# A two-stage feed-forward kernel on one Trainium2 core: the second stage's second product with its weights stationary and 512 tokens moving

## The chip, the cores and the metric

The kernel runs on one core of a Trainium2 chip. The metric is device time in microseconds of one launch; the layout of inputs before it and of outputs after it is done by the host and isn't in the time.

## What is computed

Three blocks follow each other; all data is float32.

```python
# attention without softmax, 4 x 8 heads of 576 tokens x 64
kv = einsum('bhsd,bhse->bhde', k, v)
out = einsum('bhsd,bhde->bhse', q, kv)
x = out / sqrt(mean(out * out, -1) + 1e-6) * g_norm      # -> 2304 tokens x 512
# first stage: 512 -> 1536 -> 512
x = ((x @ w_a) * (x @ w_b)) @ w_out
# second stage: 512 -> 2048 -> 512
h = x @ w_in
g = maximum(h, 0) + log1p(exp(-abs(h)))                  # softplus
return g @ w_out2
```

The change is in the last line, `g @ w_out2`.

## The kernel before

**Tokens in blocks.** The 2304 tokens are cut into five blocks. Blocks 1 to 4 are the first 512 tokens of each of the four sequences; block 0 (256 tokens) gathers the remaining 64 of each. Activations lie transposed in SBUF: features on the 128 partitions, tokens along the free axis.

**Three products for one.** Every float32 product is made of three `fp32r` products: each operand is split into a high half (ScalarE, `half_hi`, L166) and a low half, operand minus high half (VectorE, `half_lo`, L169), and `P3 = ((0, 0), (0, 1), (1, 0))` names the pairs (half of the weight, half of the operand) that are multiplied: high by high, high by low, low by high. A split tile is `[P, 2, 512]`: half, then column.

**The second stage in pairs.** Blocks 1 and 2 form pair 0, blocks 3 and 4 pair 1. Each pair is multiplied by the scheme of Strassen and Winograd with seven products of half size in place of eight. `stage1` (L608, products at L591) computes h in eight rounds i (`NCP` = 8), with `soft` for the softplus, and leaves the tiles `g2[i]`; `g_sums` on GpSimd adds and subtracts some of them. After all eight rounds of a pair, `stage2_2` (L674) does the second product. In pair 1 the rounds also hold block 0's products: `single1` (L787) and `single2` (L815), the latter through `sums` (L768).

**The stage that the change touches.** `stage2_2` runs over 56 steps: seven turns (`TURNS`: A11, S2, A12, S3, S1, A22, S4) of eight steps `cp` each. A step has one operand tile (512 tokens x 128 features, split; written by `operand`, L680) and one weight tile (128 features x 256 outputs, split). The turns add up in pairs of PSUM banks: A11 and A12 in set "a", S2, S3 and A22 in set "b", S1 and S4 in set "c". In a step the operand is the stationary side: 128 of its tokens are loaded at a time, the 256 weight columns are moved past them, and this is done for four groups of tokens (`i2`) by three halves, 12 products of 256 columns. Bank b of a set holds the tokens of groups 2b and 2b+1, 256 columns each; tokens are on the partitions of the result, as the output wants them:

```python
for i2 in range(NK):
    b, k = i2 // 2, i2 % 2
    for q, (a, c) in enumerate(P3):
        nc.tensor.matmul(out=set_[where][b][:, k * 256:(k + 1) * 256],
                         lhsT=x[:, c, i2 * P:(i2 + 1) * P], rhs=w[:, a, :], ...)
```

At the last step of a turn `leave` (L719) reads each bank out: a copy on ScalarE (L709, turns A11 and A12) or a sum with a kept tile on VectorE (L704, the others); turns A12, S1, A22 and S4 store the result by `store` (L712), two tiles of 256 KB each, in rows of 256 outputs.

**What sets the order.** Up to the first stage's start a script fixes each engine's order (`SCRIPT`); the stages behind it are written as generators, and the framework's scheduler orders each engine's instructions from what they need and from the order in which they were written. Operands are written three steps ahead (`AHEAD`). The weight tiles come from device memory, where the kernel has put the split weights (`kept`): `t_load` (L665) issues two transfers of 256 KB for two steps, on SP's queue, a turn ahead. The stores are on SP's queue too, in one row with the loads. Beside pair 0's steps `op_steps(1)` (L466) makes the operands of pair 1's first product, from step 9 to step 53 (`OPS_AT`): its sums are L480 to L482 and L499.

Of the kernel before, what the change touches and what calls it, by code (L numbers as in the profile page):

```python
# [9 lines left out]
F32 = mybir.dt.float32  # L10
# [6 lines left out]
P = 128  # L17
B, S, D = 4, 576, 64
NT = B * S
DM = 512  # L20
NK = DM // P
# [11 lines left out]
N = 512  # L33
REST = S - N
# [5 lines left out]
NCP = F2 // 2  # L40
# [70 lines left out]
def attention_gated_softplus_kernel(  # L111
# [9 lines left out]
    w2_in: bass.AP,  # L121
    w2_out: bass.AP,
    out: bass.AP,
):
    nc = tc.nc
    const = ctx.enter_context(tc.tile_pool(name="const", bufs=1))
# [13 lines left out]
    def t2(shape, dt=F32, what="t2"):  # L140
        return t2pool.tile(shape, dt, tag="t2", name=nm(what))
# [4 lines left out]
    def bank(what):  # L146
        return accp.tile([P, 512], F32, tag="acc", name=nm(what))

    def t4(shape, dt, what):
        return big.tile(shape, dt, tag="big", name=nm(what))  # L150
# [20 lines left out]
    def split(hi, lo, src):  # L171
        half_hi(hi, src)
        half_lo(hi, lo, src)
# [342 lines left out]
    def keep_steps(cp):  # L516
# [18 lines left out]
        def last(items, k, to):  # L535
# [8 lines left out]
            lambda: w_value(h[1]),  # L544
            lambda: keep((cp, 1), h[1]),
            lambda: sums(h, True),
            lambda: last(h, 0, 2),
            lambda: (last(h, 1, 2), w_load(o[0])),
# [3 lines left out]
            lambda: w_value(o[1]),  # L552
            lambda: keep((cp, 5), o[1]),
            lambda: sums(o, False),
            lambda: last(o, 0, 6),
            lambda: last(o, 1, 6),
# [108 lines left out]
    def t_load(k, half, cps):  # L665

        t = t4([P, 2, 2, 256], F32R, "w2o")
        for n, cp in enumerate(cps):
            nc.sync.dma_start(
                out=t[:, n].bitcast(F32), in_=kept_w[cp, k][:, :, half * 256:(half + 1) * 256]  # L670
            )
        return t

    def stage2_2(pair, beside):  # L674

        j1, j2 = PAIRS[pair]
        steps = [(n, cp) for n in range(len(TURNS)) for cp in range(NCP)]
        halves2, weights, set_, kept_s = {}, {}, {}, {}

        def operand(n, cp):  # L680
            name = TURNS[n][0]
            i = pair * NCP + cp
            (a11, a12), (a21, a22) = g2[i]

            src = {"A11": a11, "S2": a11, "A12": a12, "S3": a21, "A22": a22, "S4": a12}
            src = s1g[i] if name == "S1" else src[name]
            t = halves2[n, cp] = t4([P, 2, 512], F32R, "op2")
            split(t[:, 0], t[:, 1], src)
            if name == "A11":
                nc.vector.tensor_tensor(out=a11, in0=s1g[i], in1=a11, op=ALU.subtract)  # L690
            if name == "A12":
                nc.vector.tensor_tensor(out=a12, in0=a12, in1=a11, op=ALU.subtract)
            if name == "S1":
                s1g.pop(i)
            if name == "S4":
                g2.pop(i)

        def load(n, cp):
            if n < len(TURNS):
                weights[n, cp] = t_load(TURNS[n][1], TURNS[n][2], (cp, cp + 1))  # L700

        def plus(a, b):
            t = t2([P, 512], what="s2")
            nc.vector.tensor_tensor(out=t, in0=a, in1=b, op=ALU.add)  # L704
            return t

        def copy(a):
            t = t2([P, 512], what="c2")
            nc.scalar.activation(out=t, in_=a, func=AF.Copy)  # L709
            return t  # L710

        def store(j, half, b, t):  # L712
            r = (j - 1) * S + b * 2 * P
            nc.sync.dma_start(
                out=out[r:r + 2 * P, half * 256:(half + 1) * 256].rearrange("(i p) c -> p i c", p=P),
                in_=t.rearrange("p (i c) -> p i c", i=2),
            )

        def leave(name, b, o):  # L719
            if name == "A11":  # L720
                kept_s["p", b] = copy(o)
            elif name == "S2":
                kept_s["u", b] = plus(o, kept_s["p", b])
            elif name == "A12":
                store(j1, 0, b, copy(o))
            elif name == "S3":
                kept_s["v", b] = plus(o, kept_s["p", b])
            elif name == "S1":
                store(j2, 1, b, plus(o, kept_s.pop(("v", b))))
            elif name == "A22":  # L730
                store(j2, 0, b, plus(o, kept_s.pop(("p", b))))
            else:
                store(j1, 1, b, plus(o, kept_s.pop(("u", b))))

        load(0, 0)
        for x in steps[:AHEAD]:
            operand(*x)
        yield
        for cp in range(2, NCP, 2):
            load(0, cp)  # L740
        for at, (n, cp) in enumerate(steps):
            name, _, _, where, opens = TURNS[n]
            if cp == 0 and opens:
                set_[where] = [bank("acc") for _ in range(2)]
            if at + AHEAD < len(steps):
                operand(*steps[at + AHEAD])
            x, w = halves2.pop((n, cp)), weights[n, cp - cp % 2][:, cp % 2]
            for i2 in range(NK):
                b, k = i2 // 2, i2 % 2
                for q, (a, c) in enumerate(P3):  # L750
                    nc.tensor.matmul(  # L751
                        out=set_[where][b][:, k * 256:(k + 1) * 256],
                        lhsT=x[:, c, i2 * P:(i2 + 1) * P],
                        rhs=w[:, a, :],
                        start=(opens and cp == 0 and k == 0 and q == 0),
                        stop=(cp == NCP - 1 and k == 1 and q == 2),
                        skip_group_check=True,
                    )
                if cp == NCP - 1 and k == 1:
                    leave(name, b, set_[where][b])  # L760
            if cp % 2:
                weights.pop((n, cp - 1))
                load(n + 1, cp - 1)
            while beside and beside[0][0] <= at:
                beside.pop(0)[1]()
            yield

    def sums(j, i2, i, factors):  # L768
        o = bank("acc")
        for k, (a, b) in enumerate(factors):  # L770
            nc.tensor.matmul(out=o, lhsT=a, rhs=b, start=(k == 0), stop=(k == len(factors) - 1))  # L771
        if i % NCP == 0:
            total2[j, i2] = t2([P, 512], what="out")
            nc.scalar.activation(out=total2[j, i2], in_=o, func=AF.Copy)
        else:
            t = total2[j, i2]
            nc.vector.tensor_tensor(out=t, in0=o, in1=t, op=ALU.add)
            if i % NCP == NCP - 1:
                t = total2.pop((j, i2))
                for p, n in ((0, P),) if j else ((0, REST), (REST, REST)):  # L780
                    r = (j - 1) * S + i2 * P if j else (2 * i2 + p // REST) * S + N
                    nc.sync.dma_start(out=out[r:r + n, :], in_=t[p:p + n])

    total2 = {}
    B0 = BLOCKS[0]
# [38 lines left out]
    def phase2(tail):  # L824

        loaded = {0}
        second = []
        for pair in range(2):
            for i in range(pair * NCP, (pair + 1) * NCP):
                for k in range(i, min(i + 3 - pair, (pair + 1) * NCP)):  # L830
                    if k not in loaded:
                        w2_load(k)
                        loaded.add(k)
                for k, _ in enumerate(stage1(i)):
                    if i == 0 and k == 3:
                        yield from tail()
                    if k == 1 and i > pair * NCP:
                        g_sums(i - 1)
                    if k == 2 and i % NCP == NCP - 1:
                        second = stage2_2(pair, [] if pair else list(zip(OPS_AT, op_steps(1))))  # L840
                        next(second)
                    yield
                if pair:
                    yield from single1(i)
                    if i > NCP:
                        yield from single2(i - 1)
            while flow:
                advance()
            g_sums(i)
            if pair:  # L850
                yield from single2(i)
            yield from second
# [148 lines left out]
    with tc.manual_schedule(  # L1001
# [4 lines left out]
        for name in SCRIPT.split():  # L1006
            n, c, p = re.fullmatch(r"(\d*)(\D)(\d*)", name).groups()
            p = int(p) if p else None
# [35 lines left out]
    assert not any(w for _, w in todo) and done[2] == len(items)  # L1044


_OUT = (NT, DM)


# [44 lines left out]
```

## Time and profile before

| | |
|---|---|
| time, median of 3 runs (lowest to highest) | 873.33 us (872.81 to 873.74) |
| profiled execution, span from first to last instruction | 870.5 us (the page gives no other time of this execution) |
| TensorE busy | 857.5 us, 99% of the span |
| weight loads busy | 742.5 us, 85% |
| VectorE, ScalarE, GpSimd busy | 598.6, 399.2, 49.2 us |
| moved by DMA | 160.24 MB, mean 184 GB/s |
| the changed line, L751 | 1344 products, 162.5 us |

A busy time is the time in which at least one instruction of the kind ran. A product's own length contains its way through the array, which the next product overlaps; so what one product costs is read from how long an unbroken row of them takes, divided by their number.

### The profile page before, as it was taken

How to read it: one execution, taken by the hardware profiler on the slowest of the kernel's cores; microseconds unless marked ns; L12 is line 12 of the kernel's file. 1: busy time of each engine (PE TensorE's matmuls, PEld its weight loads, DVE VectorE, ACT ScalarE, POOL GpSimd, SP SyncE). 2: the span in 40 equal slices, each digit the busy share in tenths (PEclk: the TensorE clock that was granted, in tenths of full speed). 3: DMA queues.
4: the chain of work that ended last, by engine and by line, in shares of the span. 5: the costliest groups of instructions: out<-in, count | busy, mean ns of one | idle time of the engine just before them, and what ended most of it. 6: DMA issues, size and time to landing. Idle time of an engine off the chain costs nothing.

```text
span 870.5 us, 13184 instructions
## 1 busy us (share of the span) xinstructions
PE 857.5 (99%) x4972; PEld 742.5 (85%) x4972; DVE 598.6 (69%) x1045; ACT 399.2 (46%) x716; POOL 49.2 (6%) x40
## 2 busy tenths in 40 slices
PE   8999999999999999999999999999999999999998
PEld 5777788889888889888888988879999888889998
DVE  3988773448974566895663559899973667698841
ACT  5799783346742334653332323343751323246530
POOL 0000000000000000000000003420000212120000
PEclk9999999999999999999999999999999999999999
DMA  9994100258854445864422764264589844427841
GB/s 279 308 248 109 50 0 1 110 199 323 312 217 182 154 164 202 316 254 179 161 82 65 275 223 148 88 203 138 186 275 360 305 154 146 146 85 235 281 150 49
DMA packets 73007, 160.24 MB, mean 184 GB/s; under 512 B 6384, under 2 KB 41712, under 8 KB 72944
## 3 DMA queue, kind: packets, MB, share of 16 engines
q1 hardware_dynamic: 72800, 159.41, 53.9%
q8 instruction: 39, 0.64, 0.3%
q14 instruction: 24, 0.20, 0.1%
q10 hardware_dynamic: 144, 0.00, 0.0%
HBM read 121.11 MB, written 38.27 MB: 183 GB/s over the span
## 4 chain that ended last, share of the span: by engine, by line
PE 91%; DVE 4%; DMA 2%; ACT 2%; issue 1%; DVEq 0%; ACTq 0%
PE acc L751 18%; PE acc L424 16%; PE b L928 13%; PE a L928 13%; PE x L591 5%; PE v L591 5%; PE z L591 5%; PE b L957 3%; PE a L957 3%; PE h L794 3%; PE y L591 2%; PE acc L771 2%; DMA qr<-in_q_rest 1%; PE o L314 1%; DMA kvraw<-in_kv 1%; PE kvps L255 1%
## 5 line engine op out<-in xcount | busy, mean ns | idle before, releaser
L751 PE MATMUL acc<-w2o,op 128*128 128x256 f32 x1344 | 162.5, 283 | 1.6 <-DVE op L169 1.6
L751 PEld LDWEIGHTS acc<-w2o,op 128*128 128x128 f32 x1344 | 161.8, 192 | 2.4 <-DVE op L169 2.2
L424 PE MATMUL acc<-ghl,w 128*128 128x512 f32 (+1 forms) x720 | 160.9, 369 | 0.0
L928 PE MATMUL b<-x,w 128*128 128x512 f32 (+1 forms) x576 | 146.9, 363 | 0.1
L928 PE MATMUL a<-x,w 128*128 128x512 f32 (+1 forms) x576 | 146.6, 363 | 0.0
L424 PEld LDWEIGHTS acc<-ghl,w 128*128 128x128 f32 x720 | 125.6, 189 | 22.7 <-DVE y L454 0.2
L928 PEld LDWEIGHTS b<-x,w 128*128 128x128 f32 x576 | 101.8, 189 | 17.7 <-DVE w L169 0.5
L928 PEld LDWEIGHTS a<-x,w 128*128 128x128 f32 x576 | 102.0, 189 | 17.1
L393 DVE TENSOR_TENSOR g<-b,g 128x512 f32<-128x512 f32 (+1 forms) x60 | 38.1, 636 | 99.6 <-PE b L928 72.0
L389 ACT ACTIVATE g<-a 128x512 f32<-128x512 f32 (+1 forms) x60 | 33.2, 554 | 136.5 <-PE a L928 128.2
L582 ACT ACTIVATE g<-g 128x512 f32<-128x512 f32 x64 | 39.7, 631 | 100.6 <-DVE g L579 100.4
L166 ACT ACTIVATE w<-raw 128x512 fp32r<-128x512 f32 x100 | 64.7, 670 | 15.8 <-DVE raw L199 11.9
L169 DVE TENSOR_TENSOR w<-raw,w 128x512 fp32r<-128x512 f32 x100 | 66.4, 684 | 4.2 <-ACT w L166 3.9
L169 DVE TENSOR_TENSOR op<-g,op 128x512 fp32r<-128x512 f32 x96 | 63.7, 706 | 5.9 <-ACT op L166 5.6
L166 ACT ACTIVATE op<-g 128x512 fp32r<-128x512 f32 x96 | 54.6, 623 | 12.0 <-PE acc L751 10.4
L194 ACT ACTIVATE raw<-raw 128x512 f32<-128x512 f32 x68 | 46.0, 684 | 24.2 <-DMA raw<-in_w_out 18.0
L654 POOL TENSOR_TENSOR s<-g 128x512 f32<-128x512 f32 x14 | 19.6, 1402 | 633.9 <-DVE g L584 633.9
L166 ACT ACTIVATE ghl<-g 128x512 fp32r<-128x512 f32 (+1 forms) x60 | 35.3, 588 | 36.8 <-DVE g L393 34.6
L169 DVE TENSOR_TENSOR ghl<-g,ghl 128x512 fp32r<-128x512 f32 (+1 forms) x60 | 38.1, 634 | 18.5 <-ACT ghl L166 18.4
L591 PE MATMUL z<-op,w 128*128 128x512 f32 x192 | 48.9, 390 | 0.8 <-DVE c L602 0.8
L591 PE MATMUL v<-op,w 128*128 128x512 f32 x192 | 48.9, 389 | 0.0
L199 DVE SCALAR_TENSOR_TENSOR raw<-raw 128x512 int32<-128x512 int32 x68 | 46.4, 687 | 3.6 <-ACT raw L194 2.3
(103 smaller groups left out, 1090.6 us busy)
## 6 DMA issues: line engine op xcount, KB each, us to landing
w<-kept SPq DMA_DIRECT2D x80, 512.0 KB, 4.8
kept<-w SPq DMA_DIRECT2D x64, 512.0 KB, 2.9
w2o<-kept SPq DMA_DIRECT2D x112, 256.0 KB, 4.5
raw<-in_w_out SPq DMA_DIRECT2D x28, 512.0 KB, 5.2
kvraw<-in_kv SPq DMA_DIRECT2D x19, 448.0 KB, 10.5
raw<-in_w_in SPq DMA_DIRECT2D x16, 512.0 KB, 4.6
raw<-in_w_a SPq DMA_DIRECT2D x12, 512.0 KB, 7.0
raw<-in_w_b SPq DMA_DIRECT2D x12, 512.0 KB, 7.0
```

What stands on the lines that cost most here:

```text
L166: nc.scalar.activation(out=hi, in_=src, func=AF.Copy)
L169: engine.tensor_tensor(out=lo, in0=src, in1=hi, op=ALU.subtract)
L194: nc.scalar.activation(out=high_f, in_=high_f, func=AF.Prelu, scale=HIGH_SCALE, alpha=SIGN_SCALE)
L199: nc.vector.scalar_tensor_tensor(out=low, in0=high, scalar=3, in1=low, op0=ALU.logical_shift_left, op1=ALU.bitwise_or)
L389: nc.scalar.activation(out=t, in_=a, func=AF.Copy)
L393: nc.vector.tensor_tensor(out=t, in0=b, in1=t, op=ALU.mult)
L424: nc.tensor.matmul(out=acc[j][i2][:, :n], lhsT=w[:, a, c2], rhs=g[:, c, :n], start=(opens and i == 0), stop=(closes and i == 2),)
L582: nc.scalar.activation(out=to, in_=to, func=AF.Softplus)
L591: nc.tensor.matmul(out=o, lhsT=w[:, a, (2 * k + kk) * P:(2 * k + kk + 1) * P], rhs=x[:, c, :], start=(start and kk == 0 and i == 0), stop= ...
L751: nc.tensor.matmul(out=set_[where][b][:, k * 256:(k + 1) * 256], lhsT=x[:, c, i2 * P:(i2 + 1) * P], rhs=w[:, a, :], start=(opens and cp == ...
L928: nc.tensor.matmul(out=o[:, :n], lhsT=w[:, a, kk * P:(kk + 1) * P], rhs=xhl[j, kk][:, c, :n], start=(kk == 0 and k == 0), stop=(kk == NK - ...
L957: nc.tensor.matmul(out=live[x, i], lhsT=wt[x, f][:, a, kk * P:(kk + 1) * P], rhs=xhl[j, kk][:, c, :], start=(kk == 0 and k == 0), stop=(kk ...
```

## The change

`stage2_2` exchanges the two sides. The weight tile is now the stationary one, 128 outputs at a time (`b` of two), and the operand's 512 tokens move past it: 2 x 3 products of 512 columns per step. Bank b of a set now holds 128 outputs (partitions) by 512 tokens. The sums over turns, `leave`, the operands and the weight loads are as before. Since the result now has outputs on the partitions, `store` writes it transposed, to a main output of the form (4, 512 outputs, 512 tokens), in rows of 512 tokens. Block 0's sums are still made with tokens on the partitions, and go to an output of their own (4, 64, 512). The host transposes the first and joins both after the launch.

```diff
         def store(j, half, b, t):
-            r = (j - 1) * S + b * 2 * P
-            nc.sync.dma_start(
-                out=out[r:r + 2 * P, half * 256:(half + 1) * 256].rearrange("(i p) c -> p i c", p=P),
-                in_=t.rearrange("p (i c) -> p i c", i=2),
-            )
+            r = half * 256 + b * P
+            nc.sync.dma_start(out=out[j - 1, r:r + P, :], in_=t)
...
             x, w = halves2.pop((n, cp)), weights[n, cp - cp % 2][:, cp % 2]
-            for i2 in range(NK):
-                b, k = i2 // 2, i2 % 2
+            for b in range(2):
                 for q, (a, c) in enumerate(P3):
                     nc.tensor.matmul(
-                        out=set_[where][b][:, k * 256:(k + 1) * 256],
-                        lhsT=x[:, c, i2 * P:(i2 + 1) * P],
-                        rhs=w[:, a, :],
-                        start=(opens and cp == 0 and k == 0 and q == 0),
-                        stop=(cp == NCP - 1 and k == 1 and q == 2),
+                        out=set_[where][b],
+                        lhsT=w[:, a, b * P:(b + 1) * P],
+                        rhs=x[:, c, :],
+                        start=(opens and cp == 0 and q == 0),
+                        stop=(cp == NCP - 1 and q == 2),
                         skip_group_check=True,
                     )
-                if cp == NCP - 1 and k == 1:
+                if cp == NCP - 1:
                     leave(name, b, set_[where][b])
...
-                for p, n in ((0, P),) if j else ((0, REST), (REST, REST)):
-                    r = (j - 1) * S + i2 * P if j else (2 * i2 + p // REST) * S + N
-                    nc.sync.dma_start(out=out[r:r + n, :], in_=t[p:p + n])
+                for h in range(2):
+                    nc.sync.dma_start(out=out_rest[2 * i2 + h], in_=t[h * REST:(h + 1) * REST])
...
-_OUT = (NT, DM)
+_OUTS = ((B, DM, N), (B, REST, DM))
...
+    main, rest = (r.results[0][f"out_{i}"] for i in range(2))
+    return _np.concatenate([main.transpose(0, 2, 1), rest], axis=1).reshape(NT, DM)
```

The scheduler moves a few instructions with it. Three places follow; a row is a line of the kernel, the operation, the tile written and those read, the size written, and how many such follow each other.

TensorE in pair 0, steps 4 and 5 of turn A11 (`op_5` is the operand of step 4, `op_6` that of step 5; the two acc tiles are the banks of set "a"). Before:

```order
L751 MATMUL acc_5299<-w2o_5293,op_5_5317 128x256 x6
L751 MATMUL acc_5300<-w2o_5293,op_5_5317 128x256 x6
L751 MATMUL acc_5299<-w2o_5293,op_6_5336 128x256 x6
L751 MATMUL acc_5300<-w2o_5293,op_6_5336 128x256 x6
L751 MATMUL acc_5299<-w2o_5296,op_7_5352 128x256 x6
```

and now:

```order
L748 MATMUL acc_5299<-op_5_5311,w2o_5293 128x512 x3
L748 MATMUL acc_5300<-op_5_5311,w2o_5293 128x512 x3
L748 MATMUL acc_5299<-op_6_5324,w2o_5293 128x512
L748 MATMUL acc_5300<-op_6_5324,w2o_5293 128x512
L748 MATMUL acc_5299<-op_6_5324,w2o_5293 128x512 x2
L748 MATMUL acc_5300<-op_6_5324,w2o_5293 128x512 x2
L748 MATMUL acc_5299<-op_7_5334,w2o_5296 128x512 x3
```

Six products of 256 columns per bank have become three of 512; in step 5 the first products (high by high) of both banks now stand ahead of those that need the operand's low half.

VectorE in pair 0, at the end of turn S2 (step 15): the low half of step 20's operand, turn A12's subtractions, the two sums of `leave`, and the first sums of `op_steps(1)`. Before:

```order
L169 TENSOR_TENSOR op_21_5605<-g_9_4979,op_21_5605 128x512
L692 TENSOR_TENSOR g_7_4899<-g_7_4899 128x512
L692 TENSOR_TENSOR g_9_4979<-g_9_4979 128x512
L704 TENSOR_TENSOR s_1_5576<-acc_5442,c_1_5429 128x512
L704 TENSOR_TENSOR s_2_5584<-acc_5443,c_2_5437 128x512
L480 TENSOR_TENSOR s_5624<-y_1972,y_1976 128x512
```

and now:

```order
L170 TENSOR_TENSOR op_21_5503<-g_9_4979,op_21_5503 128x512
L693 TENSOR_TENSOR g_7_4899<-g_7_4899 128x512
L705 TENSOR_TENSOR s_1_5483<-acc_5394,c_1_5384 128x512
L705 TENSOR_TENSOR s_2_5488<-acc_5395,c_2_5389 128x512
L693 TENSOR_TENSOR g_9_4979<-g_9_4979 128x512
L481 TENSOR_TENSOR s_5516<-y_1972,y_1976 128x512
```

The two sums have moved ahead of one subtraction.

SP's queue in pair 0, around the stores of turn A12 (`kept_6` are weight tiles of turn S1, `kept_7` of turn S3). Before:

```order
L669 DMA w2o_5743<-kept_7_4180 128x2x256
L669 DMA w2o_5776<-kept_6_1870 128x2x256
L669 DMA w2o_5776<-kept_6_2248 128x2x256
L669 DMA w2o_5812<-kept_6_2574 128x2x256
L714 DMA out<-c_3_5731 128x2x256
L714 DMA out<-c_4_5740 128x2x256
L669 DMA w2o_5812<-kept_6_2874 128x2x256
```

and now:

```order
L670 DMA w2o_5599<-kept_7_4180 128x2x256
L670 DMA w2o_5620<-kept_6_1870 128x2x256
L715 DMA out<-c_3_5590 128x512
L715 DMA out<-c_4_5596 128x512
L670 DMA w2o_5620<-kept_6_2248 128x2x256
L670 DMA w2o_5644<-kept_6_2574 128x2x256
L670 DMA w2o_5644<-kept_6_2874 128x2x256
```

Two loads of turn S1, those of steps 33 and 34, have moved behind the two stores.

## Rows read from the trace of the kernel before

**Rows 1.** The page, its head and parts 1 and 2 (40 equal slices).

```profile
span 870.5 us, 13184 instructions
PE 857.5 (99%) x4972; PEld 742.5 (85%) x4972; DVE 598.6 (69%) x1045; ACT 399.2 (46%) x716; POOL 49.2 (6%) x40
...
PEclk9999999999999999999999999999999999999999
```

**Rows 2.** The page, part 5: line, engine, operation, tiles, count | busy us, mean ns | idle.

```profile
L751 PE MATMUL acc<-w2o,op 128*128 128x256 f32 x1344 | 162.5, 283 | 1.6 <-DVE op L169 1.6
L751 PEld LDWEIGHTS acc<-w2o,op 128*128 128x128 f32 x1344 | 161.8, 192 | 2.4 <-DVE op L169 2.2
```

**Rows 3.** The chain that ended last: start us, us, what; L751's two stretches and the end.

```profile
590.33 73.57 PE acc L751 x611
...
786.41 80.28 PE acc L751 x669
...
866.72 0.69 DVE s L704
```

**Rows 4.** The same chain: other lines with 512 columns (and L424 at 202.66 with 256).

```profile
173.34 2.72 PE acc L424 x12
...
202.66 1.44 PE acc L424 x12
...
719.02 2.75 PE acc L771 x12
```

**Rows 5.** Stretches, all engines: busy us (count) of PE, PEld, DVE, ACT, POOL; clock, DMA.

```profile
580.00:590.00 10.00, 8.78 (x66) 8.01 (x64) 9.90 (x15) 7.49 (x14) 3.03 (x2) 1.00 0.77 257
590.00:600.00 10.00, 9.67 (x80) 9.67 (x81) 10.00 (x18) 6.79 (x13) 0.00 (x0) 1.00 0.42 128
600.00:664.00 64.00, 64.00 (x535) 63.96 (x534) 47.02 (x77) 27.53 (x49) 0.00 (x0) 1.00 0.73 241
...
846.00:856.00 10.00, 10.00 (x86) 10.00 (x85) 1.38 (x2) 0.00 (x0) 0.00 (x0) 1.00 0.01 3
```

**Rows 6.** Timeline from 575 us, TensorE at pair 0's start: start us, us, what [idle before].

```profile
586.22 3.40 PE L751 MATMUL acc<-w2o,op 128*128 128x256 f32 x24 [0.84 <-DVE op L169]
587.92 1.50 PEld L751 LDWEIGHTS acc<-w2o,op 128*128 128x128 f32 x12 [0.20 <-DVE op L169]
...
590.33 9.85 PE L751 MATMUL acc<-w2o,op 128*128 128x256 f32 x80 [0.71 <-DVE op L169]
```

**Rows 7.** Timeline from 603 us, VectorE: S2's sums and what follows up to step 21.

```profile
604.05 1.28 DVE L692 TENSOR_TENSOR g<-g 128x512 f32<-128x512 f32 x2
605.62 1.41 DVE L704 TENSOR_TENSOR s<-acc,c 128x512 f32<-128x512 f32 x2 [0.29 <-PE acc L751]
...
611.43 1.29 DVE L169 TENSOR_TENSOR op<-g,op 128x512 fp32r<-128x512 f32 x2
```

**Rows 8.** The page, part 5: L424's weight loads.

```profile
L424 PEld LDWEIGHTS acc<-ghl,w 128*128 128x128 f32 x720 | 125.6, 189 | 22.7 <-DVE y L454 0.2
```

**Rows 9.** SP's issues in the timeline; w2o's landing times; the page, part 6, stores.

```profile
618.92 21.09 SPq L669 DMA_DIRECT2D w2o<-kept  x19
...
645.22 3.08 SPq L564 DMA_DIRECT2D w<-kept  x5
...
788.55 30.38 SPq L669 DMA_DIRECT2D w2o<-kept  x35
...
DMA to landing us min/median/max: 2.9/4.5/6.8
...
out<-s SPq DMA_DIRECT2D x12, 256.0 KB, 2.6
out<-out SPq DMA_DIRECT2D x4, 128.0 KB, 2.3
```

**Rows 10.** Timeline from 575 us: ScalarE's first copy, and VectorE at step 13's operand.

```profile
594.10 0.60 ACT L709 ACTIVATE c<-acc 128x512 f32<-128x512 f32 x1 [1.90 <-PE acc L751]
...
596.82 2.49 DVE L169 TENSOR_TENSOR op<-g,op 128x512 fp32r<-128x512 f32 x4
```

More of the change, by code (lines that the diff above doesn't have):

```diff
@@ L123, in attention_gated_softplus_kernel @@
     out: bass.AP,
+    out_rest: bass.AP,
 ):
@@ L1088 @@
         args.append(nc.dram_tensor(f"in_{name}", a.shape, _mybir.dt.from_np(a.dtype), kind="ExternalInput").ap())
-    args.append(nc.dram_tensor("out_0", _OUT, F32, kind="ExternalOutput").ap())
+    for i, shape in enumerate(_OUTS):
+        args.append(nc.dram_tensor(f"out_{i}", shape, F32, kind="ExternalOutput").ap())
     with _tile.TileContext(nc) as tc:
@@ L1092 @@
     r = _run(nc, [arrays], core_ids=[0])
-    return r.results[0]["out_0"]
+    main, rest = (r.results[0][f"out_{i}"] for i in range(2))
+    return _np.concatenate([main.transpose(0, 2, 1), rest], axis=1).reshape(NT, DM)
```

## The prediction

> **What bounds the kernel now.** The page first: TensorE is busy for 857.5 of 870.5 us at full granted clock in every slice, so time can leave this kernel only by giving TensorE less to do or by closing its small gaps [rows 1]. Then the groups: the line that the change rewrites, L751, is the costliest of all, 1344 products in 162.5 us with 1.6 us of waiting, and weight loads are under way for 161.8 of these 162.5 us [rows 2]. Then the chain of waits: it runs through L751 nearly without a break in both pair stages, 611 products from 590.33 to 663.90 and 669 from 786.41 to 866.69 [rows 3]. So a product that costs less there shortens the kernel one for one, unless an operand, a weight or a result then comes too late. The remaining views ask that.
>
> **The price of a product.** The second stretch gives 80.28 us / 669 = 0.1200 us for one of 256 columns, the first 73.57 / 611 = 0.1204 [rows 3]. For 512 columns the nearest row is L424, whose stationary side is a weight tile and whose moving side is an operand just split, as L751's will be: 12 products in 2.72 us, 0.2267 us each. The same line with block 0's 256 columns takes 1.44 us for 12, again 0.1200 [rows 4]. So one line at both widths shows that two products of 256 columns cost 0.2400 us and one of 512 costs 0.2267: 0.0133 us goes with every pair that becomes one. Another 512-column line, L771, shows somewhat more, 12 in 2.75 us or 0.2292 [rows 4]. I take 0.2267 and keep 0.2292 for the range.
>
> A rule of the Trainium skill speaks against so large a gain. Its page "TensorE: Matmul & The Clock Gate" (section "Back-to-back issue gap") gives a warm product N/2.4 + 2.5 ns, that is 109.2 and 215.8 ns for 256 and 512 columns. By it the change would save 672 x 2.5 ns = 1.7 us. The trace doesn't agree: it shows 120 and 227 ns.
>
> **The sum, stage by stage.** A stage has 56 steps (seven turns of eight); a step goes from 12 x 0.1200 = 1.44 us to 6 x 0.2267 = 1.36 us, 0.08 less.
> - Pair 1, 786.41 to 866.69: VectorE is busy for only 1.38 of 10 us from 846, its work nearly done while TensorE has 20 us to go, so its operands are ready long before [rows 5]. All 56 steps count: 4.48 us. That three (now two) products of step 0 are issued among block 0's last sums changes nothing in this.
> - Pair 0, steps 0 to 5: no gain up to 590.33. TensorE waits there three times for the low half of an operand, for 0.84 us, 0.20 us at the weight load, and 0.71 us [rows 6], while VectorE is busy for 9.90 of 10 us and then for all 10 [rows 5]. VectorE's work there ends when it did, and a faster TensorE waits longer. One thing moves: in step 5 the first product of the second bank now stands ahead of the wait, so that after 590.33 four products are left (0.91 us) where eleven were (1.32 us): 0.41 us.
> - Pair 0, steps 6 to 55: 50 x 0.08 = 4.00 us, if VectorE keeps up. It is busy for 10 of 10 us and then for 47.02 of 64 [rows 5]. The tightest place is step 21. Before, its low half is done at about 611.43 + 0.69 = 612.12 [rows 7]. TensorE will come to step 21 at 590.33 + 0.91 + 15 x 1.36 = 611.64 and wants the low half with the second product, at 611.87. But VectorE's chain to it also starts earlier. It began with S2's two sums at 605.62, 0.29 us after VectorE had become free, because TensorE was not yet done [rows 7]. Now TensorE reaches step 15 at 603.48 and ends its first bank by about 604.3; and the sums stand one subtraction earlier, so they can start at 604.05 + 0.60 = 604.65. The displaced subtraction follows them, so the chain gains about 0.4 us: 611.7, just in time. If it gained nothing, 0.25 us would be lost. I take none.
>
> Gain: 4.48 + 0.41 + 4.00 = 8.9 us.
>
> What else moves, and its cover. **Weight loads**: half as many LDWEIGHTS, hidden beside the products at 512 columns, where L424's loads leave 22.7 us of room [rows 8]. **w2o transfers**: same number and size. SP's order puts two of them behind A12's stores in pair 0, which wait for ScalarE's copies. Before, the queue stood there too, and went on at 618.92 [rows 9]. The longest transfer of this kind took 6.8 us [rows 9], so the two would land by about 626 at worst, and TensorE wants the first at step 33, 591.24 + 27 x 1.36 = 628.0: hidden. In pair 1 the first transfer behind block 0's stores is issued at 788.55 [rows 9]; it is turn 0's last tile, wanted at step 7, 786.41 + 81 x 0.1200 = 796.1 before and 0.6 us earlier now. Even at 6.8 us it lands at 795.4. **The next stage's tiles** `w` are issued from 645.22 [rows 9], 14 us before TensorE will want them. **ScalarE**: in pair 0 A11's two copies, the first at 594.10 before, now stand together, ahead of the operand of step 13. That one is then split by about 595.3, and VectorE came to it at 596.82 [rows 10]. **Stores**: sixteen of 256 KB, as before, in rows of 2 KB, not 1 KB. Only the last one is on the path. The nearest rows are 2.6 us (1 KB rows) and 2.3 us (128 KB in 2 KB rows) [rows 9], so -0.3 to +0.3; I take 0. **The last sum** on VectorE, 0.69 us, stays [rows 3]. Transposing the result is the host's.
>
> The profiled span is 870.5 us; the page gives no other time of that execution, and the median of the runs is 873.33, so 2.8 us lie outside the span and stay. 861.6 + 2.8 = 864.4 us.
>
> **The rivals.**
> - *Pair 0 stays held by VectorE.* For it: VectorE is full from 580 to 600 [rows 5], and step 21 has 0.2 us of margin. Against it: over the whole stage VectorE has a quarter of its time free, and TensorE waited for it only up to 590.33 [rows 5, 6]. If all of pair 0's gain went, 873.3 - 4.5 = 868.8 us; if part of it, in between.
> - *The pitch goes with the columns here.* If what makes 0.1200 us belongs to this stage's own work and not to the count of products, 512 columns take 2 x 0.1200 = 0.2400 us and nothing is gained: 873.3 us. Against it: L424 has both widths in one line [rows 4]. The page's rule named above is a mild form of this; by it the time would be 871.6 us.
> - *Slower: weight loads come into the open.* The stationary tile is now one that a transfer wrote, and three products in a row go into one bank. If a load could no longer run beside the product before it, each would cost up to its own 0.189 us (mean of L424's loads) [rows 8]. It decides from 0.0133 us per product, where it eats the gain; in full it gives 873.3 + 672 x (0.2267 + 0.189) - 161.3 = 991 us. Against it: at L424 the stationary tile is a split weight at 512 columns, and its 0.2267 us have no room for a bare load.
> - That the change doesn't do what it says is nearly excluded: the built order has products of 512 columns, three to a bank, where there were six of 256.
>
> **How the numbers follow.** What a measurement of this kernel can tell from no change is about 0.2%, 1.7 us. The forecast (gain of 6.5 to 10 us) has 0.87; pair 0 held in good part 0.06; pitch with the columns, or the page's figure, 0.04; slower 0.03. So faster 0.93, same 0.04, slower 0.03. The range: the slower pitch, 672 x (0.2400 - 0.2292) = 7.3 us, with step 21 late and no gain in step 5 leaves 6.6 us (866.7); at the other end 0.3 us off the last store and the scatter of the runs (half a microsecond to either side) give 863.4. With a little more for the scatter of a second measurement: 863.0 to 867.0 us.
>
> **What would show it.** Right: the changed line has 672 products and as many loads; the chain shows it at 0.2267 us a product; pair 1's stretch is about 75.8 us long where it was 80.28, with no wait in it; pair 0's waits for VectorE grow by a few tenths and all lie before 591; weight loads fall to about four fifths of the stage. Wrong: a product of the line at 0.23 us or more throughout; waits for VectorE after 600; a wait for a transfer at a turn's first steps; or a last store that lands much later than 2.6 us after its issue.

## The result, and the profile after

The changed kernel takes **864.07 us** (median of 4 runs, 863.58 to 864.35), the kernel before 873.07 (872.32 to 873.74) on the same chip: ratio 0.9901, 95% interval 0.9887 to 0.9915. Forecast: 864.4 us. Of all executions in this document one, of e1, took 3023 us, at full clock, and is left out of e1's ratio.

The page of the changed kernel, head, part 1, the clock of part 2, and in part 5 the changed line, now L748 (line, engine, operation, tiles, count | busy us, mean ns | idle):

```profile
span 862.5 us, 11836 instructions
PE 848.8 (98%) x4300; PEld 707.2 (82%) x4300; DVE 598.8 (69%) x1045; ACT 400.0 (46%) x716; POOL 49.1 (6%) x40
...
PEclk9999999999999999999999999999999999999999
...
L748 PE MATMUL acc<-op,w2o 128*128 128x512 f32 x672 | 153.7, 390 | 1.5 <-DVE op L170 1.5
L748 PEld LDWEIGHTS acc<-op,w2o 128*128 128x128 f32 x672 | 125.9, 188 | 28.9 <-DVE op L170 2.8
```

Beside [rows 1, 2]: 672 fewer products and loads, and TensorE is busy for 8.7 us less; VectorE, ScalarE and GpSimd do what they did. The line itself went from 162.5 to 153.7 us. Its loads, under way for nearly the whole of the line before, now leave 28.9 us free.

The chain that ended last, from the start of pair 0's second product (start us, us, what):

```profile
582.04 4.09 PE acc L748 x18
586.13 2.71 ACT op L167 x5
591.42 69.22 PE acc L748 x304
...
783.20 75.04 PE acc L748 x331
858.27 1.37 DVE s L705 x2
```

The two long stretches answer to those of [rows 3]: 69.22 us for 73.57, and 75.04 for 80.28. The second gives 75.04 / 331 = 0.2267 us a product, the price taken from L424 [rows 4].

TensorE at pair 0's start, in the timeline, columns as in [rows 6]:

```profile
587.30 3.57 PE L748 MATMUL acc<-op,w2o 128*128 128x512 f32 x13 [0.96 <-DVE op L170]
589.01 1.44 PEld L748 LDWEIGHTS acc<-op,w2o 128*128 128x128 f32 x7 [0.48 <-DVE op L170]
...
591.42 24.80 PE L748 MATMUL acc<-op,w2o 128*128 128x512 f32 x108 [0.54 <-DVE op L170]
```

The same three waits for VectorE stand here, and none follows. In this execution the first product of L748 starts at 581.87 us, before the change it was 580.79. Measured from there the last wait ends after 9.55 us, before after 9.54: VectorE sets this end, and a faster TensorE doesn't move it.

All engines in pair 0 behind those waits, and in pair 1 twenty microseconds before its end (columns as in [rows 5]):

```profile
600.00:660.00 60.00, 60.00 (x266) 49.70 (x265) 47.12 (x78) 28.10 (x51) 0.00 (x0) 1.00 0.73 243
838.00:848.00 10.00, 10.00 (x46) 8.29 (x45) 0.61 (x1) 0.00 (x0) 0.00 (x0) 1.00 0.14 54
```

TensorE is without a gap in both. The loads take 8.3 of 10 us.

**Where the time went**, one profiled execution against the other: the spans differ by 7.9 us. Pair 0, from the end of its last wait to its last product, is 69.22 us long and not 73.57: 4.35 less. Pair 1, steps 1 to 55, takes 74.96 us for 79.36: 4.40 less; its step 0 gives 0.08 more. From the last product to the end of the span it is 3.64 us, before 3.80. That makes 9.0 us. The other way goes 1.08 us which the execution after loses ahead of the stage: it has two waits there that the execution before has not, of the first stage's products for a half of a weight that is still being split, 1.1 us at 227 and 0.4 at 374. The changed kernel's other profiled executions begin pair 0's products at 580.95 and 580.43 us: what lies ahead of the stage varies by 1 us or more without any change there.

### The profile page after: what moved, and what is told of

It reads as the page before. It is cut to its first block, busy times and chain, and to the rows that moved or that the text cites. A ratio compares the mean times of both kernels' runs of the same rounds, so it can differ in the third digit from the quotient of the medians.

```text
span 862.5 us, 11836 instructions
## 1 busy us (share of the span) xinstructions
PE 848.8 (98%) x4300; PEld 707.2 (82%) x4300; DVE 598.8 (69%) x1045; ACT 400.0 (46%) x716; POOL 49.1 (6%) x40
## 4 chain that ended last, share of the span: by engine, by line
PE 88%; DVE 5%; ACT 2%; DMA 2%; issue 1%; SPq 0%; DVEq 0%
PE acc L748 17%; PE acc L425 15%; PE b L924 11%; PE a L924 11%; PE z L592 5%; PE x L592 5%; PE v L592 5%; PE a L953 4%; PE b L953 4%; PE h L790 3%; PE y L592 2%; PE acc L768 2%; DMA raw<-in_w_out 1%; PE o L315 1%; PE kvps L256 1%; DVE w L170 1%
## 5 line engine op out<-in xcount | busy, mean ns | idle before, releaser
L748 PE MATMUL acc<-op,w2o 128*128 128x512 f32 x672 | 153.7, 390 | 1.5 <-DVE op L170 1.5
L748 PEld LDWEIGHTS acc<-op,w2o 128*128 128x128 f32 x672 | 125.9, 188 | 28.9 <-DVE op L170 2.8
L390 ACT ACTIVATE g<-a 128x512 f32<-128x512 f32 (+1 forms) x60 | 33.3, 555 | 133.0 <-PE a L924 124.6
```

The costliest lines, as they stand in the source:

```text
L748: nc.tensor.matmul(out=set_[where][b], lhsT=w[:, a, b * P:(b + 1) * P], rhs=x[:, c, :], start=(opens and cp == 0 and q == 0), stop=(cp == ...
```

## The experiments

Each edits the changed kernel. "Step 0 to 6" is the time from the first product of pair 0's step 0 to that of step 6, "step 6 to the end" from there to the end of pair 0's last product, read from the single records of the trace: 10.95 and 72.16 us before the change, 10.58 and 68.18 after it.

### Is it the width, or the side? (e1, e2, e10)

Weights stay stationary, the output stays transposed, but the 512 tokens are cut: into 2 x 256 (e1), 4 x 128 (e2), 384 and 128 (e10).

e1, and e2 with four slices of 128 in the same form:

```diff
-                for q, (a, c) in enumerate(P3):
-                    nc.tensor.matmul(
-                        out=set_[where][b],
-                        lhsT=w[:, a, b * P:(b + 1) * P],
-                        rhs=x[:, c, :],
...
+                for k in range(2):
+                    for q, (a, c) in enumerate(P3):
+                        nc.tensor.matmul(
+                            out=set_[where][b][:, k * 256:(k + 1) * 256],
+                            lhsT=w[:, a, b * P:(b + 1) * P],
+                            rhs=x[:, c, k * 256:(k + 1) * 256],
```

e10:

```diff
+                for at0, at1 in ((0, 384), (384, 512)):
+                    for q, (a, c) in enumerate(P3):
+                        nc.tensor.matmul(
+                            out=set_[where][b][:, at0:at1],
+                            lhsT=w[:, a, b * P:(b + 1) * P],
+                            rhs=x[:, c, at0:at1],
```

> The weights stay stationary and the result leaves transposed, but the 512 tokens move in two rows of 256: 12 products of 256 columns a step, 1344 in all, as before the change. Theory (the gain is the number of products, 0.0133 us for each pair that becomes one): a product takes 0.1200 us again, a step 1.44 us, and the whole gain goes: 873.1 us. Rival (the gain comes from which operand is stationary, or from the stores' form): a step stays below 1.44 us, and the time stays at 864 us or comes part of the way.

Measured: 872.77 us, ratio to the kernel before 0.9999 (0.9989 to 1.0009). Its page and its chain:

```profile
L749 PE MATMUL acc<-op,w2o 128*128 128x256 f32 x1344 | 162.5, 283 | 1.6 <-DVE op L170 1.6
L749 PEld LDWEIGHTS acc<-op,w2o 128*128 128x128 f32 x1344 | 161.8, 192 | 2.4 <-DVE op L170 2.2
```

```profile
591.35 73.57 PE acc L749 x611
787.42 80.28 PE acc L749 x669
```

These are the numbers of [rows 2, 3] to the last digit, with the sides exchanged, the output transposed and the stores in rows of 2 KB. Together these three are worth nothing, within 0.1% either way; the gain is 1344 products becoming 672.

> As the changed kernel, but the tokens move in four rows of 128: 24 products a step, 2688 in all. What makes a product of 256 columns 0.1200 us? Theory A, a fixed cost beside the columns: two rows of the trace before give 0.4167 ns a column (0.2267 less 0.1200 over 256 columns) and 0.0133 us fixed, so a product of 128 columns takes 0.0667 us, a step 1.60 us, and the kernel 864.1 + 112 x 0.24 = 891 us. Theory B, a floor under each product (a product of 64 columns took about 0.112 us at L314, 36 in 4.3 us busy): a product takes 0.112 us, a step 2.69 us, and the kernel 864.1 + 112 x 1.33 = 1013 us.

Measured: 1009.3 us (one execution), span 1007.4. The chain:

```profile
581.48 150.03 PE acc L749 x1344
853.98 149.82 PE acc L749 x1342
```

150.03 / 1344 = 0.1116 us a product. The line through the two other widths, 0.0133 us + 0.4167 ns a column, gives 0.0666 for 128 columns. So rows of such products have a floor, as the forecast of 1013 us had it. At 256 columns (0.1200) the kernel before was just above it.

> Each stationary block of weights meets the 512 tokens as a product of 384 columns and one of 128: as many products as before the change, of the same total columns, with unequal widths. If a product costs a fixed part and a part per column (from 0.1200 us at 256 columns and 0.2267 at 512: 0.0133 + 0.4167 ns a column) and never less than the 0.1116 us that products of 128 columns took, one of 384 takes 0.1733 and a pair 0.2849 us; a step of six products takes 1.709 us in place of 1.36, and 112 steps add 39.1 us: 903 us. If the 0.1116 us are no floor of the single product but belong to runs of short products alone, the pair costs 0.1733 + 0.0666 = 0.2399 us, a step 1.44 us, and the time is that of the kernel before, 873 us.

Measured: 902.4 us (one execution). The chain:

```profile
590.02 88.09 PE acc L749 x611
800.67 96.30 PE acc L749 x670
```

96.30 us for 670 products are 1.725 us for the twelve of a step, forecast 1.709. As many products of as many columns in all as before the change, and 29 us slower: the narrow products cost the floor and the wide ones pay in full. Both terms of the cost hold, within 1%, for the sum of three wide and three narrow products (0.863 us, forecast 0.855), but not for the single distance from start to start. That is 0.230 us behind the first wide product and 0.175 behind the other two; behind the first narrow one it is 0.060, behind the other two 0.111 and 0.112. So 0.1116 us is no least distance of two starts; what it may be is said at the end. That the time came out at the forecast 903 us is in part luck: the steps were dearer than forecast, but steps 0 to 6 of pair 0 grew by 0.6 us only, since they wait for VectorE anyway, and this execution began the stage 1.4 us earlier.

### One pair alone (e4)

```diff
+                m = 512 if pair else 256
...
+                            rhs=x[:, c, k * m:(k + 1) * m],
```

> Pair 1 as in the changed kernel, pair 0 with the tokens in two rows of 256 (weights stationary in both). Theory (each pair's stage gives its own part, 4.4 us in pair 0 and 4.5 in pair 1): 864.1 + 4.4 = 868.5 us. Rival (pair 0 was held by VectorE and gave nothing): 864.1 us, no different from the changed kernel.

Measured: 867.8 us (867.15 to 868.36), ratio 0.9941 (0.9927 to 0.9956). The chain:

```profile
589.83 73.57 PE acc L750 x611
786.00 75.04 PE acc L750 x331
```

Pair 0 is as before the change, pair 1 as after it. By the ratio pair 1's half is worth 5.2 us (3.8 to 6.4). In the trace its stretch of the chain is 5.24 us shorter than before, but it holds 331 wide products, the work of 662 narrow ones, where it held 669; seven narrow ones are 0.84 us, and 4.40 us are left for 331 products, as in the changed kernel. The two halves of the gain stand apart and add up; the rival's time, that of the changed kernel (ratio 0.9901), lies outside the interval.

### What bounds the stage next (e3)

```diff
-                for q, (a, c) in enumerate(P3):
+                for q, (a, c) in enumerate(P3[:2]):
...
-                        stop=(cp == NCP - 1 and q == 2),
+                        stop=(cp == NCP - 1 and q == 1),
```

The product of the weights' low half by the operand's high half is left out: TensorE has a third less to do in the stage, everything else stays.

> Leaves out one of the three products of halves (low half of the weight by high half of the operand) in the second product of blocks 1 to 4, in both pairs: four products of 512 columns a step, 0.91 us instead of 1.36. It asks how far the line can still shrink before operands or weights set the pace. If TensorE alone sets it: 864.1 - 112 x 0.453 = 813 us. If VectorE takes over in pair 0 (it has about 56 us of work between 591 and 660 us, against 50 x 0.91 = 45 us of products) the gain there is 13 us, not 23: 823 to 826 us, with waits for VectorE after step 6 and perhaps for transfers at pair 1's second turn, where the smallest margin of a weight tile was 3.4 us.

Measured: 830.8 us (one execution), span 829.0. 224 products of 0.2267 us are 50.8 us; 33.3 of them came, and the 823 to 826 us of the theory that operands come next were missed. In pair 0 this theory held: the pair takes 65.7 us, 13.1 less than in the changed kernel where 13 were forecast, and from 591 to 647 VectorE is busy for 55.0 of 56 us. What it missed lies behind pair 0: pair 1 gains 22.6 of its 25.4 us, and 2.5 us more pass between the pairs, 1.1 of them in a wait for a weight tile `w` of the stage between them. TensorE in the timeline from 600 us, then ScalarE:

```profile
605.29 1.66 PE L748 MATMUL acc<-op,w2o 128*128 128x512 f32 x6 [0.83 <-DVE op L170]
611.37 23.00 PE L748 MATMUL acc<-op,w2o 128*128 128x512 f32 x87 [4.42 <-ACT op L167]
...
610.16 0.63 ACT L167 ACTIVATE op<-y 128x512 fp32r<-128x512 f32 x1 [10.03 <-DVE y L483]
```

And TensorE in pair 1:

```profile
778.64 6.31 PE L748 MATMUL acc<-op,w2o 128*128 128x512 f32 x26 [0.20 <-DMA w2o<-kept]
785.16 1.16 PE L748 MATMUL acc<-op,w2o 128*128 128x512 f32 x4 [0.22 <-DMA w2o<-kept]
787.48 12.78 PE L748 MATMUL acc<-op,w2o 128*128 128x512 f32 x54 [1.16 <-ACT op L167]
```

Operands come next, but not alone. In pair 0 the longest wait is at step 21: TensorE waits 4.4 us there for the high half of an operand. In ScalarE's queue that half stands behind a split for pair 1 (`op<-y`), and this one waits for the sums of `op_steps(1)` on VectorE (L481 to L483), while ScalarE does nothing for 10 us. And in pair 1 TensorE waits twice for a weight tile from device memory, 0.2 us each time, and once 1.2 us for the high half of an operand, behind a tile that landed 0.1 us earlier. In the changed kernel as it is the closest such transfer lands 3.4 us before its product (3.9 before the change).

The long wait has a second price, the clock. Stretches of the same trace (busy us of PE, PEld, DVE, ACT, POOL; granted clock, DMA share, GB/s):

```profile
611.00:613.00 2.00, 1.62 (x3) 1.02 (x4) 2.00 (x4) 2.00 (x5) 0.00 (x0) 0.50 0.00 0
615.00:617.00 2.00, 2.00 (x6) 1.55 (x5) 2.00 (x5) 1.06 (x2) 0.00 (x0) 0.50 0.00 0
617.00:619.00 2.00, 2.00 (x10) 1.61 (x9) 2.00 (x4) 1.75 (x5) 0.00 (x0) 0.94 0.47 181
```

After the wait TensorE runs at 1.2 GHz, half its clock, for some 6 us, and ten of its products in a row start 0.427 us apart, not 0.2267: 2 us more, behind a wait of 4.4. How much of the 2 us reaches the end isn't shown, since VectorE has hardly a free moment in this pair.

### The waits at pair 0's start (e5 to e9, e11, e12)

The changed kernel leaves 10.58 - 6 x 1.36 = 2.4 us in steps 0 to 6. Two edits go at VectorE's queue there. e6: the subtractions that prepare turn S2's operands are written behind turn A11's splits, no longer among them. e7: in the last round the two sums of `g_sums` are made on VectorE and not on GpSimd. e8: both.

e6:

```diff
+            if name == "S2":
+                nc.vector.tensor_tensor(out=a11, in0=s1g[i], in1=a11, op=ALU.subtract)
             split(t[:, 0], t[:, 1], src)
-            if name == "A11":
-                nc.vector.tensor_tensor(out=a11, in0=s1g[i], in1=a11, op=ALU.subtract)
```

e7:

```diff
+        engine = nc.vector if i == NCP - 1 else nc.gpsimd
-        nc.gpsimd.tensor_tensor(out=t, in0=a21, in1=a22, op=ALU.add)
-        nc.gpsimd.tensor_tensor(out=a21, in0=a11, in1=a21, op=ALU.subtract)
+        engine.tensor_tensor(out=t, in0=a21, in1=a22, op=ALU.add)
+        engine.tensor_tensor(out=a21, in0=a11, in1=a21, op=ALU.subtract)
```

> The changed kernel itself, as the measure for the three runs beside it on the same chip: 864.1 us. From its first changed product in pair 0 to the start of step 6 it took 10.6 us in the profile (six steps at 1.36 us are 8.2), with TensorE waiting for operands in steps 3 to 5.

> The changed kernel with A11's eight subtractions (operand line 690) written just before turn S2 splits the tile that they make, not just after A11 has read it. Theory (what still holds pair 0's first steps is VectorE's order: two subtractions stand ahead of step 5's low half): step 5's low half comes 1.2 us earlier, its wait goes, the stretch to step 6 shrinks by about 0.8 us, and the kernel takes 863.3 us. Rival (the wait is only handed on, to a later step or to S2's operands, which now cost VectorE 1.2 us a step): 864.1 us.

> The changed kernel with the two sums of pair 0's last round (lines 654 and 655) on VectorE in place of GpSimd. In the changed kernel's trace the low halves of steps 3 and 4 take 1.77 us each while these sums run on GpSimd, and 0.68 us otherwise. Theory (GpSimd's sums slow VectorE by more than they would cost it): step 3's low half comes 0.5 us earlier, the two sums cost VectorE 1.2 us in return, the stretch to step 6 shrinks by about 0.6 us: 863.5 us. Rival (VectorE is the fuller engine there, so what it takes over delays the operands): 864.1 to 865 us.

> Both edits together. If each removes a wait of its own, the stretch to step 6 shrinks by about 1.4 us and the kernel takes 862.7 us; if one wait only takes the other's place, no better than the better of the two, 863.3 us.

| kernel | time us (range) | ratio to before (interval) | step 0 to 6 | step 6 to the end |
|---|---|---|---|---|
| e5, changed kernel | 863.48 (863.25 to 865.15) | 0.9894 (0.9878 to 0.9909) | 10.58 | 68.17 |
| e6, late subtraction | 864.47 (863.52 to 865.14) | 0.9900 (0.9883 to 0.9917) | 9.80 | 69.28 |
| e7, sums on VectorE | 863.18 (862.22 to 864.75) | 0.9888 (0.9871 to 0.9905) | 9.31 | 68.51 |
| e8, both | 862.71 (862.31 to 863.65) | 0.9882 (0.9868 to 0.9897) | 8.94 | 69.08 |

By the times alone the four can't be told apart: e5's executions alone lie 1.9 us apart, and the intervals overlap. e6 missed its forecast of 863.3 us; e7 (863.5) and e8 (862.7) came near theirs, e8 in part by luck, since of 1.6 us gained at the start 0.9 came back. The trace tells more. Each edit shortens the start, and each gives some of it back behind step 6; e6 gives back more than it gained. The place is step 21 again. e8, TensorE and VectorE there:

```profile
611.03 7.34 PE L749 MATMUL acc<-op,w2o 128*128 128x512 f32 x31 [0.56 <-DVE op L170]
...
605.35 0.69 DVE L481 TENSOR_TENSOR s<-y,y 128x512 f32<-128x512 f32 x1
...
609.69 0.69 DVE L170 TENSOR_TENSOR op<-y,op 128x512 fp32r<-128x512 f32 x1
610.29 1.29 DVE L170 TENSOR_TENSOR op<-g,op 128x512 fp32r<-128x512 f32 x2
```

From 605.35 to 610.29 VectorE makes, but for one subtraction, sums and a split for pair 1, whose products begin when pair 0 is done, at 658; step 21's low half comes behind them. So e9 is e8 with them later, by the table that places `op_steps`:

```diff
-OPS_AT = [9, 13, 17, 21, 25, 29, 33, 36, 39, 42, 47, 49, 51, 53]
+OPS_AT = [9, 13, 23, 26, 29, 31, 33, 36, 39, 42, 47, 49, 51, 53]
```

> Beside the late subtraction and the sums on VectorE, the S2 half's sums of the second stage (the OPS_AT table, VectorE adds that the seventh product's operands wait for) are put behind A12's operands, so that step 21 of pair 0 should not wait again. Theory (the waits at pair 0's start are VectorE's queue, and what e8 gave back at step 21 was its queue once more): steps 0 to 6 take 8.9 us as in e8, and step 6 to the stage's last product 68.2 us as in the changed kernel; about 0.9 us under e8 and 1.6 us under the changed kernel, 862.0 to 862.6 us. Rival (the wait only moves on, to the next turn's operands, since VectorE's work up to there is the same): step 6 to the end stays at 69 us with the wait behind step 21, and the time is 862.7 to 863.5 us.

> The changed kernel once more, as the measure beside e9: 863.5 to 864.5 us, 0.989 to 0.990 of the kernel before, steps 0 to 6 of pair 0 in 10.6 us and step 6 to the last product in 68.2 us.

Measured: e9 862.74 us (861.81 to 862.78), ratio 0.9885 (0.9869 to 0.9902); e11, the changed kernel on the same chip, 862.95 (862.42 to 863.85), 0.9889 (0.9874 to 0.9903). By the times alone the two can't be told apart, and both missed their forecasts: e9's median lies in the rival's range, e11's under its own. e9 in the timeline of TensorE and in the chain:

```profile
580.96 4.70 PE L749 MATMUL acc<-op,w2o 128*128 128x512 f32 x20
585.90 32.48 PE L749 MATMUL acc<-op,w2o 128*128 128x512 f32 x141 [0.24 <-DVE op L170]
```

```profile
585.90 72.14 PE acc L749 x316
780.68 75.04 PE acc L749 x331
```

One wait of 0.24 us is left in the pair. Step 0 to 6 takes 8.92 us and the rest 68.16: 77.08 in all, 78.74 in e11, 1.65 us less, as forecast. But in that execution the stage began 0.5 us later than in e11, by what varies ahead of it. So the kernel ran once more:

> The kernel of e9 once more, since its single executions (861.81 to 862.78 us) overlap the changed kernel's (862.42 to 863.85) in the same call, though its stage was 1.65 us shorter in the trace. Theory (the 1.65 us reach the end, and what lies ahead of the stage varies from one execution to the next by about as much): pair 0's products take 77.1 us again against 78.7 in the changed kernel, the median over both runs of this kernel is 861.9 to 862.8 us, 1.0 to 1.7 under the median of the changed kernel's three runs (863.5). Rival (what the waits at pair 0's start give, a later transfer or store takes back): pair 0 as short, but the median at 863.2 to 863.8.

Measured: 861.56 us (861.23 to 862.08), ratio 0.9866 (0.9850 to 0.9883); pair 0 again 8.93 + 68.16 us. The eight executions of this kernel have their median at 861.96 us, the twelve of the changed kernel (this section's and the result's) at 863.55: 1.6 us less, what the trace shows in pair 0. Times of different chips are mixed in this, so the trace is the better witness.

## Why the prediction was right

- **The price of a product.** 0.2267 us was taken from L424, and 0.2267 it is. e1 shows that nothing but number and width of the products made the gain. The rival in which the pitch goes with the columns is out.
- **The page's rule.** The traces show 0.1116, 0.1200 and 0.2267 us for products of 128, 256 and 512 columns. The Trainium skill ("TensorE: Matmul & The Clock Gate", section "Back-to-back issue gap") gives 55.8, 109.2 and 215.8 ns by N/2.4 + 2.5, which it calls the gap of an isolated product, and about 81 and 131 ns for 128 and 512 columns in a stream of weight loads and products. At no width of this kernel does the trace agree with either.
- **Pair 1**: 56 x 0.08 = 4.48 us forecast, 4.48 measured (4.40 and 0.08 for step 0). The chain's stretch is 75.04 us and not the 75.8 that was named as a sign, because it holds 331 products where half of the 669 before would be 334 or 335.
- **Pair 0, steps 0 to 5**: 0.41 forecast from the moved product; step 0 to 6 went from 10.95 to 10.58, 0.37. Not all waits grew (0.84 to 0.96, at the load 0.20 to 0.48, but the last from 0.71 to 0.54), since the moved products stand ahead of the last one now.
- **Pair 0, steps 6 to 55**: 4.00 forecast; 72.16 to 68.18 us, 3.98. That VectorE holds pair 0 was the first rival; it didn't come, by the margin at step 21, below.
- **Loads.** Not exposed: 125.9 of 153.7 us, the four fifths that were forecast. The slower rival is out.
- **Transfers.** SP's queue in the changed kernel, at turn A12's stores:

```profile
617.11 1.35 SPq L715 DMA_DIRECT2D out<-c  x2
618.51 20.09 SPq L670 DMA_DIRECT2D w2o<-kept  x21
```

  The loads behind the stores were issued from 618.51; before, the queue went on at 618.92 [rows 9]. Step 33 began at 629.2 without a wait, 6.5 us after its tile had landed. In pair 1 the first tile behind block 0's stores landed 3.7 us before its product.
- **The last store**, taken as 0: from its issue to its landing 1.99 us, before 2.15.
- **Outside the span: the mis-sized term.** The prediction set 873.33 against a span of 870.5 and so put 2.8 us outside. The profiled execution of the changed kernel has 864.35 us by a span of 862.5: 1.85 outside. So the 870.5 belonged to an execution of about 872.4 us, faster than the three runs whose median was used (872.81 to 873.74), and the sum made from the profile should have ended at 863.5. The profiled execution's 864.35 holds the 1.08 us that it lost ahead of the stage, and the two nearly cancel: that the forecast lies only 0.3 us from the median of this result is in part luck. The changed kernel's twelve executions have their median at 863.55. Of the difference of the medians, 9.0 us, 8.9 was forecast. The range has a slip of its own: 0.3 and 0.5 us off 864.4 give 863.6, not 863.4. This result lies in the range, 863.0 to 867.0; e11's 862.95 lies just under it.

**Step 21**, the place that the prediction called tight. VectorE in the changed kernel's timeline:

```profile
605.73 1.28 DVE L705 TENSOR_TENSOR s<-acc,c 128x512 f32<-128x512 f32 x2
...
611.98 1.29 DVE L170 TENSOR_TENSOR op<-g,op 128x512 fp32r<-128x512 f32 x2
```

The two sums start without the pause of [rows 7], behind one subtraction fewer, as forecast. The low half is done at 611.98 + 0.69 = 612.67; step 21 begins at 612.88 and wants it with its second product, at 613.1. The forecast had 0.17 us of room, the trace has 0.4. That little was left there e6 to e8 show: whenever TensorE came 0.8 to 1.6 us earlier, it waited.

## What to carry to other kernels

Price a product by unbroken rows of them in the kernel's own trace, at each width, and look for a line that has both widths: here a fixed 0.0133 us per product, and a floor of 0.1116 in rows of narrow ones, made the widest product the cheapest per column. A stage that TensorE fills takes such a gain one for one only as far as the in-order queues of the engines that feed it allow; find the step with the least room before the change, and see what work for later stands in the queue ahead of it. Where the forecast is a sum on a profiled span, take the time outside the span from an execution that has both.

## What the runs showed of the hardware beyond that

- **Rows of narrow products have a floor of 0.1116 us** at 128 columns (e2), beside weight loads that last 0.19 us each and overlap. The traces point at the load as its cause. Behind a wide product, beside which its weights are loaded, the first narrow one lets the next start after 0.060 us (128 columns, e10) or 0.028 to 0.031 us (64 columns, L314 of the kernel before); further on in the row the distance is 0.111 to 0.112 us at either width. No run takes the loads away, so this is argued and not shown.
- **At half the clock the fixed part isn't seen.** There a product of 512 columns takes 0.427 us (e3), which is twice 0.2133: nothing is left of the fixed 0.0133 us that it pays at full clock. What this fixed part is made of stays open.
- **During a wait of TensorE of 4.4 us its granted clock fell** to 0.50 and stayed there for some 6 us behind it (e3). Behind the waits of 0.5 to 1 us at pair 0's start in the changed kernel it stayed at 1.00.
- **VectorE is slowed by GpSimd.** In the changed kernel, VectorE and GpSimd during the waits at pair 0's start:

```profile
585.30 1.40 POOL L655 TENSOR_TENSOR s<-g 128x512 f32<-128x512 f32 x1 [7.49 <-DVE g L585]
586.78 1.63 POOL L656 TENSOR_TENSOR g<-g,g 128x512 f32<-128x512 f32 x1
...
585.48 3.48 DVE L170 TENSOR_TENSOR op<-g,op 128x512 fp32r<-128x512 f32 x2
590.68 1.28 DVE L170 TENSOR_TENSOR op<-g,op 128x512 fp32r<-128x512 f32 x2
```

Two low halves take 3.48 us beside GpSimd's two sums, and 1.28 us without them. e7, which moves these two sums to VectorE, gives it more to do; the low half of step 3 takes 0.68 us there, and steps 0 to 6 take 9.31 us, not 10.58. The Trainium skill ("GPSIMD Engine Reference", section "1. Specifications") says that GpSimd's way to SBUF is shared with VectorE, with contention for VectorE's operations of two SBUF inputs, as the low half is; the trace agrees, 1.74 us for 0.64 each.
